# First x chunk as two 64-row halves on two queues, and the gate vector behind the first wk piece: a change to the opening loads of a tuned kernel

## The chip, the cores and the metric

One core of one Trainium2 chip. The metric is the device time of one execution in microseconds (us); lower is better. Executions of the kernel before agree within 0.4% in each batch. Times inside a trace are counted from the start of the profiled span, which is about 1.7 us shorter than the device time (264.4 against 266.17 us in the kernel before).

The engines: PE is TensorE, DVE VectorE, ACT ScalarE, POOL GpSimd, SP SyncE. SP and ACT each issue DMAs into a queue of their own, here called the SP queue and the ACT queue; the profile counts 16 DMA engines for the core. The trace has the data of these loads in packets of 256 or 1280 bytes, each with its start, here called the time at which it is read, and reports of completion: 16 for each load of 64 or 128 rows, on either queue (for x chunk 0 in the kernel before from 2.64 to 3.08), and 6 for the gate vector. Here a load has landed with the last of its reports. A transposing load turns rows into columns on its way; the others are called plain copies.

## The reference, cut to what matters

```python
g = sigmoid((x * gate_w).sum(-1))            # x: 2048 x 640, gate_w: 640
a = linear_attention(x, wqkv, wo)            # k = x @ wk, then phi(k) = exp or t + 1
b = mlp_mixer(x, w1, w2, w3, w4)
out = g * a + (1 - g) * b
```

The kernel gets the gate's logit (the value inside the sigmoid) for one more column: it appends gate_w as column 640 of wk, so that the matmuls for k also give x . gate_w.

## The kernel before: the opening

```python
load_x(0, 1)                                                        # SP: chunk 0, 128 rows
aq.dma_start(g5[:], gate_w.rearrange("(c p) -> c p", p=P))          # ACT: the gate vector, 5 x 128
load_wk(sp, 1)
load_wk(aq, 0)
load_wk(aq, 2)
load_wk(sp, 3)
load_wk(aq, 4)                                                      # wk in five pieces of 128 rows
for c0, c1 in ((1, 2), (2, 3), (3, 4), (4, 6), (6, 8), (8, 12), (12, 16)):
    load_xT(c0, c1)                                                 # SP: transposing loads of the other chunks
# ... (further loads on SP cut)
warmup(6)                              # 6 matmuls of 512 columns and 3 of 128, on constants
warmup(3, P)
for n, (ptb, a, b) in enumerate(turns):                             # turns: pieces 0-1, then 2-4
    for dc in range(a, b):
        nc.tensor.transpose(ptb[:, ...], x_sb[:, 0, dc * P:(dc + 1) * P], ident[:])
    nc.vector.tensor_copy(xT[:, a:b, 0:P], ...)
    if n == 0:                         # between x's second and third transpose
        nc.tensor.transpose(tg[:, 0:DC], g5[:], ident[0:DC, 0:DC])
        nc.vector.tensor_copy(wk_sb[:, :, D], tg[:, 0:DC])
warmup(3, P)
for dc in range(DC):                   # chunk 0 of k: wk pieces in the order 0, 1, 2, 3, 4
    k_mm(kp, 0, (dc,))
    if dc < DC - 1:
        warmup(1, 2 * P)
k_evac(kp, 0)                          # ACT copies the logit (ylog), then phi
for c in range(1, NCH):                # chunks 1 to 15 come from the transposing loads
    # ... (cut)
```

PE keeps to the program's order: in the trace after the change, x's third transpose, whose data landed at 3.38, runs at 6.87, right behind the gate's at 6.76, which waited for the gate vector. And x and wk pieces 1 and 3 stand on the SP queue ahead of the transposing loads.

## Time and profile before

| | before |
|---|---|
| device time, fast runs beside the change | 266.3, 266.48, 266.91 us |
| profiled span | 264.4 us |
| PE busy | 98% |

The page of the kernel before: the span, busy time by engine, and the engines' shares of the chain that ended last.

```profile
span 264.4 us, 4255 instructions
PE 259.7 (98%) x1744; PEld 162.2 (61%) x1744; DVE 139.3 (53%) x270; ACT 85.1 (32%) x126; POOL 20.2 (8%) x55
...
PE 91%; SPq 3%; DMA 3%; ACT 1%; issue 0%; DVE 0%
```

PE is the bottleneck (98% busy), so a loss at the start is paid in full unless PE would have waited later anyway. The chain in order of time (start, length, what) shows such a wait:

```profile
7.64 1.67 SPq L121
...
9.35 6.94 DMA xT<-in_A_x_dram
16.29 0.05 issue
16.34 11.07 PE pp L190 x80
```

SP's issues of transposing loads lead to the load of chunks 8-11, which lands at 16.29; from there on it is PE alone. The timeline of PE in the kernel before (start, length, instructions):

```profile
3.66 0.42 PE L211 MATMUL pp<-ident,x_sb 128*128 128x128 bf16 x2
4.01 0.18 PE L214 MATMUL pp<-ident,g 5*128 5x5 bf16 x1
4.13 0.36 PE L211 MATMUL pp<-ident,x_sb 128*128 128x128 bf16 x3
...
4.73 0.43 PE L190 MATMUL pp<-wk_sb,xT 128*128 128x320 bf16 x2
```

None of these lines ends in a wait in brackets: x's transposes stand behind the warm-up, the gate's behind them. ACT's copies of the logit show when each chunk of k is done (the bracket is ACT's own idle time, no loss); chunks 0, 1, 7 and 8:

```profile
6.74 0.16 ACT L194 COPY ylog<-pp 128x1 f32<-128x1 f32 x1 [2.72 <-PE pp L190]
8.14 0.16 ACT L194 COPY ylog<-pp 128x1 f32<-128x1 f32 x1 [0.64 <-PE pp L190]
...
16.32 0.16 ACT L194 COPY ylog<-pp 128x1 f32<-128x1 f32 x1 [0.59 <-PE pp L190]
17.91 0.16 ACT L194 COPY ylog<-pp 128x1 f32<-128x1 f32 x1 [0.82 <-PE pp L190]
```

Chunks take 1.36 us each, but 1.59 from chunk 7 to chunk 8: the 0.23 us by which PE waits for the load that lands at 16.29.

What the DMA engines moved, in windows of one microsecond (for each: busy time of the five engines, then granted PE clock, mean busy share of the DMA engines, GB/s; the share is the sum of the packets' times, and passes 1 where these overlap, as in the 1.23 here):

```profile
5.00:6.00 1.00, 1.00 (x10) 0.78 (x8) 0.00 (x0) 0.00 (x0) 0.73 (x6) 1.00 1.23 265
6.00:7.00 1.00, 1.00 (x10) 0.61 (x8) 0.00 (x0) 0.26 (x2) 0.93 (x3) 1.00 1.07 228
```

### The profile page before, as it was taken

What the parts mean: (1) busy time and instruction counts of PE and PEld (TensorE: products, weight loads), DVE (VectorE), ACT (ScalarE), POOL (GpSimd) and SP (SyncE); (2) the same over time, 40 slices, a digit from 0 to 9 for tenths busy, and PEclk for the clock granted to TensorE, in tenths of its full rate; (3) what the DMA queues carried; (4) which work ended last, traced back from release to release, by engine and by line L of the source; (5) the groups of instructions that cost most, each with busy time, mean ns of one, the idle gap of its engine ahead of it and who ended that gap; (6) DMA issues with size and microseconds to landing.
All of it is one profiled execution on the core that took longest, in us unless ns stands there. A gap on an engine that the chain in (4) does not pass through costs nothing.

```text
span 264.4 us, 4255 instructions
## 1 busy us (share of the span) xinstructions
PE 259.7 (98%) x1744; PEld 162.2 (61%) x1744; DVE 139.3 (53%) x270; ACT 85.1 (32%) x126; POOL 20.2 (8%) x55
## 2 busy tenths in 40 slices
PE   8999999999999999999999999999999999999994
PEld 4767555788755644555667555667565667455762
DVE  1788688899858588955403464503455313112132
ACT  1555444321165636622502212312131422233000
POOL 7100010012300140001000001000001000000000
PEclk9999999999999999999999999999999999999999
DMA  7999978015673727600132000042000041100011
GB/s 202 184 211 365 377 222 318 0 43 121 128 92 68 78 51 193 207 0 2 25 74 77 25 0 2 0 99 75 26 0 2 1 99 58 44 0 2 0 59 40
DMA packets 46093, 23.61 MB, mean 89 GB/s; under 512 B 35451, under 2 KB 45435, under 8 KB 46075
## 3 DMA queue, kind: packets, MB, share of 16 engines
q1 hardware_dynamic: 45632, 22.86, 34.0%
q10 hardware_dynamic: 442, 0.49, 0.5%
q8 instruction: 13, 0.21, 0.3%
q14 instruction: 6, 0.04, 0.1%
HBM read 12.21 MB, written 2.62 MB: 56 GB/s over the span
## 4 chain that ended last, share of the span: by engine, by line
PE 91%; SPq 3%; DMA 3%; ACT 1%; issue 0%; DVE 0%
PE pp L479 22%; PE pp L460 21%; PE pp L307 8%; PE pp L413 8%; PE pp L444 8%; PE pp L341 8%; PE pp L232 8%; PE pp L190 4%; SPq L121 3%; DMA xT<-in_A_x_dram 3%; PE pp L468 1%; PE pp L488 1%; ACT m_sb L381 1%; PE pp L360 1%; PE pp L247 0%; SPq L124 0%
## 5 line engine op out<-in xcount | busy, mean ns | idle before, releaser
L460 PE MATMUL pp<-lnxT,w_sb 128*128 128x512 bf16 x260 | 60.4, 379 | 0.0
L479 PE MATMUL pp<-w_sb,h 128*128 128x256 bf16 (+1 forms) x416 | 57.9, 299 | 0.0
L462 ACT ACTIVATE h<-pp 128x1024 bf16<-128x1024 f32 (+1 forms) x28 | 26.9, 961 | 82.2 <-PE pp L460 82.2
L479 PEld LDWEIGHTS <-h 128*128 128x128 bf16 x416 | 40.3, 98 | 16.6 <-issue 1.1
L460 PEld LDWEIGHTS <-w_sb 128*128 128x128 bf16 x260 | 25.4, 98 | 26.8
L495 DVE SCALAR_TENSOR_TENSOR oc<-pp,omg,x 128x640 bf16<-128x640 f32 x15 | 12.9, 882 | 44.0 <-ACT h2x L471 21.3
L447 DVE SCALAR_TENSOR_TENSOR x<-pp,gate,x 128x640 f32<-128x640 f32 x16 | 13.9, 868 | 29.4 <-PE pp L444 29.4
L416 DVE TENSOR_TENSOR x<-pp,x_sb 128x640 f32<-128x640 f32 x16 | 13.1, 820 | 22.6 <-PE pp L413 22.6
L182 ACT ACTIVATE e<-pp 128x640 bf16<-128x640 f32 (+1 forms) x26 | 21.5, 826 | 9.6 <-PE pp L232 9.6
L444 PE MATMUL pp<-m_sb,pqT 128*128 128x320 bf16 x160 | 24.3, 299 | 0.0
L413 PE MATMUL pp<-w_sb,hsT 128*128 128x320 bf16 x160 | 23.9, 299 | 0.1
L190 PE MATMUL pp<-wk_sb,xT 128*128 128x320 bf16 (+1 forms) x160 | 22.6, 300 | 0.1
L307 PE MATMUL pp<-x_sb,pk 128*128 128x320 bf16 (+1 forms) x160 | 22.3, 300 | 0.0
L232 PE MATMUL pp<-xT,hsT 128*128 128x512 bf16 x100 | 21.7, 379 | 0.0
L307 PEld LDWEIGHTS <-pk 128*128 128x128 bf16 x160 | 18.8, 117 | 3.5
L413 PEld LDWEIGHTS <-hsT 128*128 128x128 bf16 x160 | 15.6, 98 | 8.2 <-issue 0.2
L444 PEld LDWEIGHTS <-pqT 128*128 128x128 bf16 x160 | 15.7, 98 | 7.7
L190 PEld LDWEIGHTS <-xT 128*128 128x128 bf16 x160 | 15.4, 98 | 6.4 <-DMA xT<-in_A_x_dram 0.6
L341 PE MATMUL pp<-lnxT,w_sb 128*128 128x512 bf16 x80 | 17.9, 379 | 0.0
L232 PEld LDWEIGHTS <-hsT 128*128 128x128 bf16 x100 | 11.8, 118 | 9.7
L277 POOL TENSOR_SCALAR rstd<-mv 128x4 f32<-128x4 f32 (+1 forms) x11 | 3.4, 313 | 156.5 <-DVE mv L283 156.5
L184 DVE SCALAR_TENSOR_TENSOR pk<-pp,e 128x640 bf16<-128x640 f32 x16 | 13.2, 825 | 1.7
(77 smaller groups left out, 191.6 us busy)
## 6 DMA issues: line engine op xcount, KB each, us to landing
out_dram<-oc SPq DMA_DIRECT2D x15, 160.0 KB, 1.8
w_sb<-in_B_w_dram SPq DMA_DIRECT2D x1, 2160.0 KB, 8.4
w_sb<-in_B_w_dram SPq DMA_DIRECT2D x1, 2080.0 KB, 10.0
x_sb<-in_A_x_dram SPq DMA_DIRECT2D x2, 640.0 KB, 10.7
x_sb<-in_A_x_dram SPq DMA_DIRECT2D x1, 1120.0 KB, 8.2
wo_sb<-in_A_wo_dram SPq DMA_DIRECT2D x6, 160.0 KB, 8.3
hsT<-in_A_wqkv_dram SPq DMA_DIRECT2D x1, 800.0 KB, 5.7
m_sb<-in_A_wqkv_dram SPq DMA_DIRECT2D x1, 800.0 KB, 11.5
```

The lines of the kernel that those rows point to most:

```text
L182: nc.scalar.activation(ev, src, ACT.Exp)
L184: nc.vector.scalar_tensor_tensor(dst, src, 0.0, ev, op0=ALU.max, op1=ALU.add)
L190: nc.tensor.matmul(pt[:, hf, 0:n], lhsT=xT[:, dc, c * P:(c + 1) * P], rhs=wk_sb[:, dc, hf * HD:hf * HD + n], start=(dc == 0), stop=(dc == ...
L232: nc.tensor.matmul(pt[:, t % 2, :], lhsT=wq_sb[:, dc, :].rearrange("p (m j) -> p j m", j=DC)[:, j], rhs=xT[:, dc, t * TS:(t + 1) * TS], st ...
L307: nc.tensor.matmul(pt[:, hf, 0:HD + hf], lhsT=w, rhs=x_sb[:, c, hf * HD:(hf + 1) * HD + hf], start=(c == 0), stop=(c == NCH - 1))
L341: nc.tensor.matmul(pt[:, i, :], lhsT=w, rhs=lnxT[t][:, dc, :], start=(dc == 0), stop=(dc == DC - 1))
L413: nc.tensor.matmul(pt[:, hf, 0:HD], lhsT=hsT[:, fc, 2 + c * P:2 + (c + 1) * P], rhs=w2_sb[:, fc, hf * HD:(hf + 1) * HD], start=(fc == 0), ...
L444: nc.tensor.matmul(pt[:, hf, 0:HD], lhsT=pqT[:, j, c * P:(c + 1) * P], rhs=m_sb[:, j, hf * HD:(hf + 1) * HD], start=(j == 0), stop=(j == D ...
L447: nc.vector.scalar_tensor_tensor(x1, pt[:, :, 0:HD], gate[:, c:c + 1], x1, op0=ALU.mult, op1=ALU.add)
L460: nc.tensor.matmul(pt[:, k, :], lhsT=w3_sb[:, dc, fc * P:(fc + 1) * P], rhs=lnT[:, dc, :], start=(dc == 0), stop=(dc == DC - 1))
L462: nc.scalar.activation(h2[:, 2 * i * TS:(2 * i + n) * TS], pt[:].rearrange("p h e -> p (h e)")[:, 0:n * TS], ACT.Gelu_apprx_tanh)
L479: nc.tensor.matmul(dst, lhsT=st[t]["h2"][:, fc * TS + cc * P:fc * TS + (cc + 1) * P], rhs=w4_sb[:, fc, a:b], start=start and fc == 0, stop ...
```

## The change

The intent: x chunk 0 sooner, since each queue brings half of it and nothing is ahead of either half; and wk piece 0 sooner, since the gate vector no longer stands ahead of it.

```diff
-    load_x(0, 1)
-    aq.dma_start(g5[:], gate_w.rearrange("(c p) -> c p", p=P))
+    for q, r0 in ((sp, 0), (aq, P // 2)):
+        q.dma_start(x_sb[r0:r0 + P // 2, 0, 0:D], x2[r0:r0 + P // 2, :])
     load_wk(sp, 1)
     load_wk(aq, 0)
+    aq.dma_start(g5[:], gate_w.rearrange("(c p) -> c p", p=P))
     load_wk(aq, 2)
     load_wk(sp, 3)
     load_wk(aq, 4)
```

## The prediction

> **What bounds the kernel now.** TensorE. The page gives PE 98% busy of 264.4 us at a clock of 0.998; the chain that ended last is 91% PE. Only its first 16.3 us are not: in the chain in order of time, SyncE's DMA issues run from 0.79 to 9.31 us (x chunk 0 and two wk pieces, 0.40 to 0.42 each, then transposing loads of x, 1.27 to 1.67 each), then 6.94 us for the load of chunks 8-11, landing at 16.29; after that PE alone.
>
> **The head, by timeline and landing events.** Warm-up matmuls occupy PE from 0.83 to about 3.56. x chunk 0's last engine reported at 3.08. PE's transposes (weight load at 3.56, no idle before it) do not wait for x but stand behind the warm-up. The gate vector, issued at 0.79, landed at 2.14; PE transposes it at 4.01, between the second and third transpose of x, unwaited. wk piece 0, issued at 1.39, landed at 4.68; the first k matmul ran at 4.73.
>
> **What the change moves.**
> - x in halves: same 160 KB, same 16 DMA engines. [...] I expect x 0.1-0.4 us earlier, worth nothing: PE is in warm-up until 3.56.
> - wk piece 0: half of x is ahead of it instead of the gate vector; landing about 4.3-4.7. Worth 0 to 0.2 us.
> - Gate vector: issued about 1.7 instead of 0.79. [...] the 256-byte packets of the first transposing load, issued at 2.18, start only at 4.75, when the 1280-byte ones of wk are done. So the gate vector lands behind wk piece 0, at about 4.2-4.7. PE executes in order: its transpose goes from 4.01 to 4.4-4.8 and holds the other transposes of x, the DVE copies (0.17 and 0.36 us) and the first k matmul. The head loses 0.3-0.6 us.
> - One more DMA: semaphores are reused after eight, with a wait for the earlier landing (in the trace from the second transposing load on). wk piece 4 or the first transposing load will now wait for a half of x; if the load, all transposing loads go 0.3-0.6 us later, straight onto the chain.
>
> **What reaches the end.** k evictions follow each other every 1.36 us, but 1.59 where chunk 8 begins: PE waits 0.23 us there for its load (and about 0.04 for chunk 1). A late head is swallowed up to about 0.26 us. The load's landing stays at 16.3 (SyncE issues the same number of DMAs). Net 0 to +0.35 us, up to +0.6 in the bad semaphore case, -0.25 at best: +0.15 on about 266.6 (fast runs 266.17 to 266.91).
>
> **Predicted: 266.8 us, 266.0 to 267.6. Faster by over 2%: 0.01; within 2%: 0.97; slower: 0.02.**
>
> **What would show it.** x landing before 3.1 with PE's first transpose still at 3.56; the gate vector landing after 4.1 and PE waiting before its transpose; first k matmul at 5.0-5.3; the wait at chunk 8 shrunk or gone; everything behind shifted by under 0.5 us.
>
> **What would make it wrong.** The gate vector's data slipping ahead of wk piece 0's; wk, not DVE, having held the first k matmul, so that its earlier arrival pays; transposing loads moving by over 0.3 us.

The sum came to 0 to +0.35 us: 0.3 to 0.6 us lost in the head, of which up to 0.26 are swallowed at chunk 8; +0.6 in the semaphore case and -0.25 at best. The +0.15 put on about 266.6 gives the 266.8. The packets of 256 and 1280 bytes named are those of the SP queue. What it says of semaphores is seen in the trace before: eight serve the DMAs, and the ninth DMA, the second transposing load (issued at 3.52), waits on that of the gate vector, landed at 2.14.

## More of the kernel before

Before, SP carries 480 KB of plain copies ahead of the transposing loads and ACT 480 KB. After, it is 400 and 560.

## The result, and the profile after

| | before | after |
|---|---|---|
| device time, median | 266.7 us | 270.76 us (270.07 to 271.04) |
| ratio of the fast runs | | 1.0154, 95% interval 1.0123 to 1.0184 |
| profiled span | 264.4 us | 269.3 us |

A ratio is the mean time of one kernel's fast runs over that of the other's in the same rounds, so it is not quite the ratio of the medians. The change costs 4.1 us (1.5%, clear of the noise); the profiled execution is one of the slower ones (271.04) and shows 4.9 us more span. The prediction said 266.8, at most 267.6.

PE's timeline after the change, the lines that answer to those of before:

```profile
3.66 0.42 PE L212 MATMUL pp<-ident,x_sb 128*128 128x128 bf16 x2
6.76 0.18 PE L215 MATMUL pp<-ident,g 5*128 5x5 bf16 x1 [2.68 <-DMA g<-in_gate_w_dram]
6.87 0.50 PE L212 MATMUL pp<-ident,x_sb 128*128 128x128 bf16 x3
...
7.49 0.74 PE L191 MATMUL pp<-wk_sb,xT 128*128 128x320 bf16 x2
```

The gate's transpose waits 2.68 us for the gate vector. And x's first transpose starts at 3.66 as before, as it is still behind the warm-up. The chain, which no longer passes through the transposing loads:

```profile
1.39 0.86 ACTq L124
2.24 0.03 issue
2.27 4.44 DMA g<-in_gate_w_dram
6.71 0.05 issue
6.76 0.18 PE pp L215
6.94 0.43 PE pp L212 x3
7.37 0.32 PE pp L203 x3
7.69 0.53 PE pp L191 x2
...
10.69 21.73 PE pp L191 x152
```

The gate vector, 1.2 KB, was issued at 2.27, after wk piece 0's issue, and took 4.44 us to land, at 6.71. There is a second loss, easily missed: "7.69 0.53 PE x2" is 0.265 us for each k matmul. Before, they took 0.135 (a pair's start to the next instruction's, 4.73 to 5.00, is 0.27). PE is at half clock. ACT's copies of the logit for chunks 0, 1 and 2:

```profile
11.26 0.16 ACT L195 COPY ylog<-pp 128x1 f32<-128x1 f32 x1 [6.09 <-PE pp L191]
13.38 0.16 ACT L195 COPY ylog<-pp 128x1 f32<-128x1 f32 x1 [1.36 <-PE pp L191]
14.74 0.16 ACT L195 COPY ylog<-pp 128x1 f32<-128x1 f32 x1 [0.60 <-PE pp L191]
```

With these the account closes:

| stretch | before | after | difference |
|---|---|---|---|
| start of the gate's transpose | 4.01 | 6.76 | +2.75, the wait |
| from there to chunk 0's logit | 2.73 | 4.50 | +1.77, half clock |
| chunk 0 to chunk 1 | 1.40 | 2.12 | +0.72, half clock |
| chunk 7 to chunk 8 | 1.59 | 1.37 | -0.22, a wait swallowed |
| last logit copied | 27.45 | 32.45 | +5.00 |

So 2.75 us are the wait, 2.49 half clock, and 0.22 are given back, in these two executions. The trace's clock events agree: full clock is granted from 4.20 us before, and only from 12.64 after; the events' other value is 0.5. (The page's row of the granted clock and the windows' clock column show full clock in both, as the trace holds no clock event before the first rise; only the length of the matmuls and the time of that first event show it.)

Why did the gate land so late? The trace holds each DMA packet's start and each report of completion. Last report of each of the opening DMAs:

| | before | after |
|---|---|---|
| x chunk 0 | 3.08 | 3.10 and 3.38 |
| gate vector | 2.14 | 6.71 |
| wk pieces 0, 2, 4 (ACT queue) | 4.68, 5.47, 5.95 | 5.75, 8.49, 8.99 |
| wk pieces 1, 3 (SP queue) | 4.49, 5.27 | 4.22, 7.11 |
| first transposing load: first packet, landing | 4.90, 6.52 | 4.16, 9.10 |

Not only the gate is late: from 5 us on everything is. The same windows as before, and the next two:

```profile
5.00:6.00 1.00, 0.00 (x0) 0.00 (x0) 0.00 (x0) 0.17 (x1) 0.73 (x6) 1.00 0.89 121
6.00:7.00 1.00, 0.24 (x3) 0.23 (x4) 0.02 (x1) 0.00 (x0) 0.93 (x3) 1.00 1.17 146
7.00:8.00 1.00, 1.00 (x8) 0.79 (x7) 0.52 (x2) 0.00 (x0) 0.51 (x1) 1.00 1.23 159
8.00:9.00 1.00, 1.00 (x6) 0.61 (x5) 0.00 (x0) 0.00 (x0) 0.00 (x0) 1.00 1.12 166
```

The DMA engines count as busy as before, but move 121 to 166 GB/s instead of 228 to 265. In that stretch transposing packets of the SP queue and plain packets of the ACT queue are on the engines together.

### The profile page after: what moved, and what is told of

It reads as the page before. It is cut to its first block, busy times and chain, and to the rows that moved or that the text cites. A ratio compares the mean times of both kernels' runs of the same rounds, so it can differ in the third digit from the quotient of the medians.

```text
span 269.3 us, 4258 instructions
## 1 busy us (share of the span) xinstructions
PE 262.1 (97%) x1744; PEld 163.6 (61%) x1744; DVE 139.4 (52%) x270; ACT 85.1 (32%) x126; POOL 20.1 (7%) x55
## 4 chain that ended last, share of the span: by engine, by line
PE 95%; DMA 2%; ACT 1%; ACTq 1%; DVE 0%; issue 0%
PE pp L480 21%; PE pp L461 21%; PE pp L191 9%; PE pp L308 8%; PE pp L414 8%; PE pp L445 8%; PE pp L342 8%; PE pp L233 8%; DMA g<-in_gate_w_dram 2%; PE pp L469 1%; PE pp L489 1%; ACT m_sb L382 1%; PE pp L361 1%; PE pp L248 0%; PE pp L203 0%; ACTq L124 0%
## 5 line engine op out<-in xcount | busy, mean ns | idle before, releaser
L191 PE MATMUL pp<-wk_sb,xT 128*128 128x320 bf16 (+1 forms) x160 | 24.9, 317 | 0.0
L191 PEld LDWEIGHTS <-xT 128*128 128x128 bf16 x160 | 16.5, 104 | 7.1
L184 DVE TENSOR_SCALAR e<-e 128x640 bf16<-128x640 bf16 (+1 forms) x26 | 9.5, 365 | 10.5 <-ACT e L183 9.0
```

Source lines behind the costliest of these rows:

```text
L191: nc.tensor.matmul(pt[:, hf, 0:n], lhsT=xT[:, dc, c * P:(c + 1) * P], rhs=wk_sb[:, dc, hf * HD:hf * HD + n], start=(dc == 0), stop=(dc == ...
```

## The experiments

Each experiment ran beside the kernel before on the same chip; ratios are to that. The diffs are against the change, except those of e4, e5 and e10, which are against the kernel before. Each has four executions, one of them profiled. "ORDER", "OVERLAP", "CLOG" and "HALVES" are the theories.

First came two theories. ORDER: the gate stands behind wk piece 0, and PE waits in order. OVERLAP: the transposing loads now start while ACT's copies are under way, and both suffer.

### e1_halves_gate_first: halves kept, gate first again

```diff
+    aq.dma_start(g5[:], ...)
     for q, r0 in ((sp, 0), (aq, P // 2)): ...     # halves as in the change
     load_wk(sp, 1)
     load_wk(aq, 0)
-    aq.dma_start(g5[:], ...)
     load_wk(aq, 2)
```

> The x halves stay, but the gate vector is again the first DMA on the ACT queue. ORDER theory (the loss comes from PE waiting in order for a gate vector that lands behind wk piece 0): the gate lands near 2.2 us, PE never waits for it, and the time is back at 266.3 to 267.2. OVERLAP theory (the loss comes from the transposing loads of the SP queue starting, at about 4.0 us, while the ACT queue still has hundreds of KB of plain copies, which slows both): wk pieces 2 and 4 still land after 7 us (before: 5.47 and 5.95; after: 8.49 and 8.99), PE now waits for them instead, and the time is 269 to 271.

Measured: 267.97 us, ratio 1.0058 (1.0034 to 1.0082). The gate landed at 2.14, and a loss of 1.5 us stayed. The profile's list of waits (total, times, longest) and its chain:

```profile
PE pp L191 <- DMA wk_sb<-in_A_wqkv_dram: 1.1, 1, 1.1
...
PE pp L212 <- DMA x_sb<-in_A_x_dram: 0.4, 1, 0.4
```
```profile
3.08 5.09 DMA wk_sb<-in_A_wqkv_dram
8.17 0.04 issue
8.21 20.87 PE pp L191 x152
```

wk piece 4 landed at 8.17, where OVERLAP wanted it after 7 (piece 2, at 6.10, was not that late). ORDER alone falls. OVERLAP's 269 to 271 is missed as well: this leaves 1.5 of 4.1 us. The chain runs through piece 4, so the 0.4 us that PE waited for the second half of x lie inside this loss.

### e2_whole_x_gate_late: only the gate moved

```diff
-    for q, r0 in ((sp, 0), (aq, P // 2)): ...
+    load_x(0, 1)
     load_wk(sp, 1)
     load_wk(aq, 0)
     aq.dma_start(g5[:], ...)                      # stays behind wk piece 0
```

> x chunk 0 whole on SP as before; only the gate vector is moved behind wk piece 0 on ACT. ORDER: the gate lands behind wk piece 0, so PE waits for it and most of the loss is there: 269 to 271. OVERLAP: the SP queue still drains at about 4.7 us and the ACT queue, with no half of x on it, no later than 5.3, so the gate lands before 4.2 without a held-up completion, and the time is 266.2 to 267.2.

Measured: 266.85 us, ratio 1.0010 (0.9993 to 1.0026). The gate behind wk piece 0 landed at 4.02 and cost nothing that can be measured. So each half of the change alone costs 1.5 us or nothing, and both together 4.1: they act on each other.

### e3_halves_wk4_on_sp: the change, with wk piece 4 on SP

```diff
     load_wk(sp, 3)
-    load_wk(aq, 4)
+    load_wk(sp, 4)
```

> The change as it is, except that wk piece 4 goes on the SP queue ahead of the transposing loads instead of on ACT, so that SP holds 560 KB of copies and ACT about 400. ORDER: the gate stands behind the same wk piece 0 and half of x, so it lands as late as in the change (6.7 us) and the time stays 269.5 to 271. OVERLAP: ACT has drained when the transposing loads start (about 5 us); the gate lands at 4.0 to 4.8, wk piece 2 before 5.5, the time is 266.5 to 267.6 (one more SP issue of 0.4 us ahead of the transposing loads adds up to 0.4).

Measured: 268.09 us (267.11 to 268.51), ratio 1.0052 (1.0025 to 1.0080): half a microsecond over OVERLAP's range and well under ORDER's. The gate stands in the same place of the ACT queue as in the change, and landed at 5.30 instead of 6.71; piece 4 at 6.45. Neither was as early as OVERLAP said (gate by 4.8; piece 2 before 5.5, measured 6.65), and PE still waits:

```profile
5.34 0.17 PE L215 MATMUL pp<-ident,g 5*128 5x5 bf16 x1 [1.26 <-DMA g<-in_gate_w_dram]
```

Taking ACT's copies out of the transposes' way gives back about two thirds of the loss. The profiled execution was the fastest of the four, so the slower three stay unexplained.

### e4_before_wk3_on_act: overlap made in the kernel before

```diff
     load_wk(aq, 2)
-    load_wk(sp, 3)
+    load_wk(aq, 3)
```

> The kernel before, except that wk piece 3 goes on the ACT queue, so that SP holds only 320 KB ahead of the transposing loads and ACT 640 KB. No half of x, gate vector first. ORDER: gate at 2.2 us, nothing waits for it; the pieces [...] land at most 1 us later; 266.5 to 267.6. OVERLAP: the transposing loads start at about 3.7 to 4.0 us beside some 300 KB of copies on ACT, wk pieces 3 and 4 land after 7.5 us, PE waits for them, and the time is 268.5 to 271.

Measured: 266.84 us, ratio 1.0009 (0.9985 to 1.0032). OVERLAP missed. The transposing loads did start at 3.98, with 328 of ACT's packets still to come, and yet 264 GB/s were moved and piece 4 landed at 6.86. In this run the first transposing load was read by 5.3, and the second one's packets came only from about 6 on; in between the copies went on alone. So the theory was narrowed to CLOG: it takes both kinds together for longer ("more than about half a microsecond"), without such a pause. That doesn't quite cover e4 either: until 5.3 both kinds were together for over a microsecond, and the window from 4 to 5 moved 273 GB/s. The rival, HALVES: the 64-row transfers themselves are slow.

### e5_all_wk_on_act: long overlap without halves or a late gate

```diff
     load_x(0, 1)                                  # whole, on SP
     aq.dma_start(g5[:], ...)                      # first on ACT
-    load_wk(sp, 1); load_wk(aq, 0); load_wk(aq, 2); load_wk(sp, 3); load_wk(aq, 4)
+    for dc in range(5): load_wk(aq, dc)
```

> Whole x on SP, gate vector first on ACT, and all five wk pieces on ACT, so that the transposing loads follow x at once on SP: the plainest way to keep transposing loads and plain copies in flight together, with no half of x and no late gate. CLOG theory (revised: both kinds together on the engines for more than about half a microsecond, with no pause in the transposes, move 140 to 210 GB/s instead of some 300, and packets of plain copies take 0.2 us and more): the last wk pieces land after 8 us, PE waits for them, 268.5 to 272. HALVES theory (it is the 64-row transfers that are slow, whatever lies beside them): no 64-row transfer here, wk piece 4 lands by about 7, 266.5 to 268.

Measured: 271.85 us, ratio 1.0183 (1.0150 to 1.0215), no less than the change's whole loss (the intervals overlap), with neither half of the change in it. PE waits for wk pieces four times:

```profile
PE pp L190 <- DMA wk_sb<-in_A_wqkv_dram: 2.0, 4, 0.6
```

The last pieces landed at 8.27 and 9.36, as CLOG said; the rate while both kinds were there, 221 GB/s, lies a little above its 140 to 210. But the last piece was also issued late (4.67): in the profile's chain this issue waits for piece 0, which landed at 4.65. So this run alone proves less than its time suggests. The clock events show full clock from 6.06, half from 9.47, full again from 12.88.

### e6_after_pe_kept_busy and e12_after_pe_busy_6: is the half clock a cost of its own?

```diff
         if n == 0:
+            warmup(12)        # e6; e12 has warmup(6)
             nc.tensor.transpose(tg[:, 0:DC], g5[:], ident[0:DC, 0:DC])
```

> The change as it is, with 12 more warm-up matmuls of 512 columns (2.6 us at full clock) between the second transpose of x and the gate's, so that PE is busy while it waits for the gate vector. If the half-speed k matmuls after the wait (0.265 us instead of 0.135 between starts) come from PE having idled, they run at full speed now, the first k eviction comes near 9.4 to 9.7 us instead of 11.26 (wk piece 4, landing at 9.0, now sets it) and the time is 268.6 to 269.4. If they have another cause, the time stays at 270.3 to 271.

> The change with 6 filler matmuls instead of the 12, which overshot: they still ran at half speed until 5.97 us and kept PE until 7.69, 1.5 us after the gate had landed. With 6 (about 2.4 us) PE reaches the gate's transpose near 6.5. If the clock's late rise is worth about 2.4 us of the change's loss, the full clock comes at 6 to 8, the first k eviction at 8.9 to 9.6 (11.26 in the change, 10.23 with 12) and the time is 268.6 to 269.6, faster than with 12. If the filler has nothing more to give: 269.8 to 271.

Ten matmuls of the fillers' 512 columns take 2.16 us at full clock in the chain of the change. With 12 fillers: 269.97 us, ratio 1.0116 (1.0095 to 1.0136). The k matmuls ran at full speed, but the time missed the range: the fillers themselves were slow until the clock rose at 5.97, and kept PE until 7.69 though the gate had landed at 6.16. With 6: 268.57 us, ratio 1.0080 (1.0053 to 1.0108), at the edge of the range expected. Its PE timeline:

```profile
3.88 2.62 PE L203 MATMUL pp<-const-bfloat16-1.0 128*128 128x512 bf16 x6
6.87 0.17 PE L216 MATMUL pp<-ident,g 5*128 5x5 bf16 x1 [0.37 <-DMA g<-in_gate_w_dram]
...
7.49 0.43 PE L191 MATMUL pp<-wk_sb,xT 128*128 128x320 bf16 x2
```

The gate landed as late as in the change (6.82), but PE had something to chew on: full clock from 6.23, chunk 0's logit at 9.51 instead of 11.26. The loss is 2.1 us instead of 4.1, each beside its own runs of the kernel before, with the DMAs untouched. So 2.0 us is the half clock's part, measured by itself (2.49 by the account above, of one execution).

### e7_whole_x_on_act: more imbalance, no halves

```diff
-    for q, r0 in ((sp, 0), (aq, P // 2)): ...
+    aq.dma_start(x_sb[:, 0, 0:D], x2[0:P, :])
```

> x chunk 0 whole, but on the ACT queue; the gate behind wk piece 0, everything else as in the change. SP holds 320 KB of copies, ACT 640 KB, so the imbalance is larger than in the change (400 and 560), without 64-row transfers. CLOG: the gate's completion is held up beside the first transposing load (after 5 us), wk pieces 2 and 4 land after 7, 268.5 to 272. HALVES: gate by 4.8, wk piece 4 by 6.6, 266.5 to 267.8.

Measured: 269.33 us, ratio 1.0099 (1.0078 to 1.0120). No 64-row transfer, and the gate (5.71), piece 2 (7.05) and piece 4 (8.11) are all late: CLOG's numbers, not HALVES'. The chain has the gate's 4.00 us from issue to landing:

```profile
1.72 4.00 DMA g<-in_gate_w_dram
```

(Piece 4 was also issued late, at 4.30, behind the landing of x; the gate and piece 2 were not.)

### e8_halves_both_on_sp: halves without imbalance

```diff
-    for q, r0 in ((sp, 0), (aq, P // 2)): ...
+    for q, r0 in ((sp, 0), (sp, P // 2)): ...
```

> x chunk 0 as two 64-row transfers, both on SP; ACT as in the run with the whole x and a late gate (wk piece 0, gate, 2, 4). SP and ACT hold 480 KB each. CLOG: ACT has drained by about 5.7, before the transposing loads come in number; gate at about 4.0, wk piece 4 by 6.4; one more SP issue delays the transposing loads by about 0.5, so 266.7 to 267.6. HALVES: the 64-row transfers are slow here too, with x landing after 3.9 and a PE wait of over 0.5 us, or a slow stretch of the engines between 4.5 and 8 us as in the change: 268 to 270.

Measured: 269.0 us (267.21 to 269.07), ratio 1.0065 (1.0031 to 1.0099). No slow stretch: gate at 3.47, piece 4 at 6.01. The loss is another one: the second half could be issued only at 1.40, after an issue of 0.56 us, and landed at 4.60. The profile's chain around it:

```profile
4.39 0.30 POOL emat L163
4.70 0.04 issue
4.73 0.37 PE pp L212 x2
...
6.05 0.54 PE pp L191 x2
```

PE's transposes of x start at 4.73 instead of 3.66, and the k matmuls run at half clock (full clock from 10.13). The POOL operation named as the releaser is an inference of the profile that does not fit, as the transposes do not read what it writes; the half of x that landed at 4.60 does. By the letter HALVES is met: time, x after 3.9, a wait of 0.86 us. What this run lacks is the slow stretch: 370 and 318 GB/s in the windows 4 to 5 and 5 to 6. The late issue explains 0.6 us of the late x; why the second half then took 3.20 us from issue to landing, against 2.29 for the whole chunk before, is open.

### e9_after_plain_xT and e10_before_plain_xT: the same packets, not transposing

Both are wrong: chunks 1 to 3 are loaded without transposing. (They still passed the comparison with the reference, whose tolerance three such chunks of sixteen do not break.)

```diff
     def load_xT(c0, c1):
-        sp.dma_start_transpose(xT[:, :, c0 * P:c1 * P], x2[c0 * P:c1 * P, :])
+        if c1 <= CPT:
+            sp.dma_start(xT[:, :, c0 * P:c1 * P], x2[c0 * P:c1 * P, :].rearrange("p (c s) -> p c s", c=DC))
+        else: ...                                  # transposing as before
```

> Wrong result on purpose. The change as it is, but the loads of x chunks 1 to 3 on SP are plain loads of the same bytes in the same number of 256-byte packets, not transposing ones (the later chunks still transpose). If it is the transposing that holds up the plain copies beside it: the gate, read near 4.2 to 4.7, lands by 5.1, wk pieces 2 and 4 land by 7, PE's wait for the gate falls from 2.7 to under 1 us, and the time is 266.6 to 268. If any small packets beside the ACT queue's copies do it (queue sharing, 64-row halves, the gate's place): gate after 6, wk piece 4 after 8, 269.5 to 271.

> Wrong result on purpose; the control for the run before it: the kernel before with the same plain loads of chunks 1 to 3. Little overlapped with ACT's copies there, so I expect no more than the small waits at chunks 1 and 8 to change: 266.0 to 266.9.

The control: 266.42 us, ratio 0.9985 (0.9966 to 1.0004), so the edit does nothing to the kernel before. On the change: 268.09 us, ratio 1.0059 (1.0018 to 1.0100); two executions at 267.2, two at 268.9 and 269.4, of which the profiled one is a fast one. Its chain's line for the gate (4.44 in the change), and its windows, to be set against the change's 121, 146, 159:

```profile
2.27 3.25 DMA g<-in_gate_w_dram
```

```profile
5.00:6.00 1.00, 0.43 (x4) 0.32 (x5) 0.18 (x1) 0.17 (x1) 0.73 (x6) 1.00 1.09 302
6.00:7.00 1.00, 1.00 (x11) 0.81 (x10) 0.36 (x1) 0.00 (x0) 0.93 (x3) 1.00 0.92 241
7.00:8.00 1.00, 1.00 (x11) 0.75 (x9) 0.00 (x0) 0.00 (x0) 0.54 (x1) 1.00 1.16 240
```

The packets have the same size, number and queue, but in this execution the slow stretch is gone. Pieces 2 and 4 landed at 6.31 and 7.31 (8.49 and 8.99 in the change). The gate landed at 5.53, better than 6.71 but not at the 5.1 expected: its last packet was read only at 4.99, then reported after 0.53. So the first theory's numbers are all missed by a little (piece 4 by 7, a wait under 1 us, 268 at most) and the rival's (gate after 6, piece 4 after 8, 269.5 and more) by much. Beside many small plain packets the gate is late too, and a wait of 1.5 us is left; but the slow stretch comes with the transposing. The two slow executions have no trace.

### e11_after_gate_on_pool: the gate taken off the ACT queue

```diff
-    aq.dma_start(g5[:], gate_w.rearrange("(c p) -> c p", p=P))
+    gq.dma_start(g5[:], gate_w.rearrange("(c p) -> c p", p=P))
```

> The change, with the gate vector issued from GpSimd instead of behind ACT's wk piece 0; ACT has one issue less. If the late gate was all of the loss: 266.3 to 267.2. If the transposing loads also hold up the wk pieces, as in the run with the halves and the gate first: gate by 4.0, but wk piece 4 lands after 7 and PE waits for it; 267.2 to 268.6.

Measured: 268.15 us, ratio 1.0055 (1.0037 to 1.0072). The gate landed at 4.13 (expected by 4.0), so that PE hardly waited for it, and piece 4 at 8.71:

```profile
PE pp L191 <- DMA wk_sb<-in_A_wqkv_dram: 1.4, 2, 1.1
```

As in e1, with the gate out of the way by another route: 1.6 us of loss remain, in the wk pieces.

### What holds the gate up

The gate's five packets and their reports, by run; "transposing packets" are those of 256 bytes on SP that had started before the gate's last report (in e9, 633 plain packets of that size had started instead). Of the runs left out, e1, e4, e5 and e10 have the gate first, as before; no transposing packet had started by its report:

| run | packets read | last report | from last read to last report | transposing packets by then |
|---|---|---|---|---|
| before | 1.72-1.80 | 2.14 | 0.34 | 0 |
| e8 | 2.69-2.78 | 3.47 | 0.69 | 0 |
| e2 | 3.07-3.36 | 4.02 | 0.66 | 0 |
| e11 (GpSimd's queue) | 3.18-3.51 | 4.13 | 0.62 | 0 |
| e3 | 4.37-4.73 | 5.30 | 0.57 | 16 |
| e9 (plain) | 4.28-4.99 | 5.53 | 0.53 | 0 |
| e7 | 3.95-4.14 | 5.71 | 1.57 | 596 |
| e6 | 4.27-4.70 | 6.16 | 1.46 | 562 |
| e12 | 3.86-4.54 | 6.82 | 2.28 | 588 |
| the change | 4.14-4.63 | 6.71 | 2.08 | 530 |

The gate was read about when predicted, at 4.14 to 4.63. What was late is the report, at 6.71. From the last read to the last report the table has 0.34 to 0.69 us with at most 16 transposing packets started by then, and 1.46 to 2.28 with 530 to 596. What held the report back is not shown; no run separates the possible causes.

From the first packet of the SP queue's loads of chunks 1-3 to the last of ACT's copies, the engines moved 165 GB/s in the change and 285 in e9, with mean times of ACT's packets of 141 and 58 ns. The median is 55 ns in both, so a minority is very slow: 60 of 267 packets took over 0.2 us in the change, 3 of 272 in e9. Over e1, e5, e7 and e11 the rate was 217, 221, 209 and 172. It differs between executions, too: e6 and e12 have the change's DMAs, and moved 229 and 173. What the slow ones share is that ACT still had 209 packets or more to come when the first transposing packet started; where it had 121 or fewer (before, e2, e3, e8) the rate was 264 to 334. e4, with 328 and 264 GB/s, is the exception.

## Why the prediction was wrong

- **PE bound, head only, x's halves worth nothing: right.** x's first transpose stayed at 3.66 (3.56 with its weight load, from which the prediction counts). That the halves would be 0.1 to 0.4 us earlier was wrong: 3.38 for the later one, against 3.08, with issues of 0.56 us each instead of one of 0.40, and 0.86 instead of 0.37 for ACT's next issue (wk piece 0). Each half has 16 reports, as the whole chunk has.
- **The gate behind wk piece 0, PE held in order: right in mechanism, wrong in size, and this is the step that failed.** That it "lands behind wk piece 0, at about 4.2-4.7" took the reading for the landing. It landed at 6.71, and the wait was 2.75 us instead of 0.3-0.6. The missed term is about 2.1 us between read and report, with 530 transposing packets started by then. The trace before showed no such gap: there the gate's last report came 0.34 us after its last read. (The order on the SP queue held: in the kernel before the first transposing packet started at 4.90, not the 4.75 of the prediction, after the last wk packet of its queue, 4.78.)
- **"The load's landing stays" and wk pieces 2 and 4 left out of the sum: wrong.** The load of chunks 8-11 landed at 17.62 instead of 16.29, which cost nothing, as PE came to chunk 8 later still. What cost time were ACT's copies: with more ahead of them and issued later, they ran until 8.39 instead of 5.40, beside transposing loads that started at 4.16 instead of 4.90. The earlier start is not needed for it: in e1 these loads started at 4.95, and ACT's copies still ran until 7.42. The prediction treated the queues as if only the order within each mattered. Without a late gate this alone costs 1.5 us (e1, e11).
- **The clock was no term of the sum at all.** It cost 2.0 us (e12) to 2.49 (the account). In the change PE idled before its clock had been raised (2.68 us ahead of the gate's transpose), and full clock came at 12.64 instead of 4.20. That the idling did it is shown for the change: with PE kept busy and the DMAs as they were, the rise came at 6.23 (e12).
- **How much clock a wait costs is partly luck, which no prediction from one trace can know.** In all traces the clock's rises and falls lie whole multiples of 3.413 us apart (259.413 us, 76 windows, in the kernel before; 256.000, 75, in the change; 6.06, 9.47 and 12.88 in e5). From these spacings comes an estimate: windows of 3.413 us, counted back from each trace's rise and laid over PE's matmuls (whose ends are modelled). So counted, the clock rose at the end of a window with at most 0.66 us of idling (e7; 0.46 in e3, whose wait of 1.3 us lay for the rest behind the rise at 4.54), and stayed low after 0.84 (e7), 0.86 (e8) and, in the change, 1.73 (2.40 to 5.81) and 0.95 (5.81 to 9.22). The fall has no edge as clean: once up, the clock fell after a window with 1.72 us of idling (e5, at 9.47, with no wait over 0.63 us), but not after 1.40 (e11), nor after 1.76 at the end of e9. Where the windows fall differs from execution to execution: the opening of the kernel before had its rise at 4.20 in one trace and, with e10's edit, which cost nothing, at 6.24. And in two of the change's four executions the recorded mean clock is 0.991 and 0.992 instead of 0.999 and 0.998. By an estimate, 0.991 over 268.8 us is 4.8 us at half clock: a window of 3.41 after a first rise, as in e5, and the end of the span. These two took 270.51 and 270.07 us, the others 271.0; they have no trace.
- **The late head swallowed up to 0.26 us: right,** 0.22.
- **The ninth DMA's semaphore wait: right, and harmless.** wk piece 4's issue waited from 3.24 to 3.40 for a half of x, landed at 3.38.

What stays open: why e4, with the transposing loads starting as early and more copies to come, clogged so little (264 GB/s; the pause in its transposes is what the trace shows, but no run makes or removes that pause alone); what happens inside the DMA engines; and why e3, e8 and e9 vary by 1.4 to 2.2 us between executions. For the last, a late rise of the clock has about the right size (2.0 to 2.49 us in the change), and the shifting windows would bring it in some executions only, but no trace of both kinds exists. No version here beats the kernel before.

## What to carry to other kernels

Before moving bytes from one DMA queue to another, ask what both queues will have on the engines at the same time: here ACT's plain copies became longer by 80 KB, ran on beside SP's transposing loads, and the engines moved 121 to 166 GB/s instead of 228 to 265. A small load can be read early and still be late: the gate vector's 1.2 KB were read by 4.63 and reported at 6.71, and PE's transpose of it started at 6.76. So keep what PE waits for in the midst of its program away from transposing traffic. And early in a kernel a wait of PE may have to be paid twice: once for itself, and once for the clock that it keeps low. It was so in the change (2.7 us of waiting, and 2.0 to 2.49 of half clock), not in the profiled executions of e3 and e9 (1.3 and 1.5).
